# Subtracting the low halves of the inner groups on POOL instead of DVE, in a chain of attention and two mixtures

## The chip, the cores and the metric

One Trainium2 chip, one core of it. The metric is the device time of one execution in microseconds; for the kernel before, the median of three runs is 637.03 us (636.54 to 637.32).

## The reference

An attention-like scan over 4 x 8 heads of 768 positions, then two feed-forward layers over the 3072 tokens of 256 features:

```python
x = attn_out.transpose(0, 2, 1, 3).reshape(B * S, H * D)      # 3072 x 256
h = x @ w_in                                                  # 256 -> 2048
g = maximum(h, 0) + alpha * minimum(h, 0)
x = g @ w_out                                                 # 2048 -> 256
gate = 1 / (1 + exp(-(x @ w_gate)))                           # 256 -> 1536
out = (gate * (x @ w_val)) @ w_out2                           # 1536 -> 256
```

## The kernel before, in words

All matrix products of the two layers are made in pieces, to keep float32 accuracy: each operand is split into a high half, which is a rounded copy, and a low half, which is the operand minus that copy. A product is then high x high, low x high and high x low. The weights are split once, in seven small operations per block (`work`, lines 142 to 185, called through `feed`); their raw words come by DMAs issued from POOL's queue (`take_up`, line 126), each of which waits until the buffer of an earlier block is free, that is until DVE has done line 181 of that block.

Tokens go in 6 blocks of 512, named `k`; the inner features go in groups of 128, named `f`. One step (k, f) of the first mixture has on PE six matmuls into `h` (`moe1_in`, line 429), on ACT the first half of the activation (`t`, line 434), on DVE the second half (`g`, line 436), and then `halves` (lines 441 to 452): ACT copies `g` into the high half `gh` (line 449), DVE subtracts it and leaves the low half `gl` (line 450). `moe1_out` (line 473) gives `gh` and then `gl` to PE, four and two matmuls. In the second mixture the inner value is `p`, and `moe2_out` has lines 552 (with `gh`) and 557 (with `gl`).

The order of the work is written out by hand, and each engine takes its instructions strictly in that order. There are three stages:

- The attention, in 32 chunks of 96 positions, into which the first 26 steps of the first mixture are woven; these call `halves` at line 935.
- The loop of lines 979 to 1003: the other steps of the first mixture and the first block of the second, 82 steps. Step i has `halves` of step i - 1, the inner products of step i and the outer products of step i - 2 (`LAG = 2`), then two weight operations. `halves` is called at line 981.
- `moe2_pair` (lines 659 to 736), for the blocks k = 1 to 5 of the second mixture, six pairs of groups j = 0 to 5 for each: 30 calls. It makes the inner products of two groups with seven products instead of eight, into the PSUM banks `a`, `b` and `c`, with DVE forming sums between them (lines 681, 694, 695, 718, 721) and the two values `p0` (lines 696 and 727) and `p1` (line 725). `halves(before[0])` of line 686 splits the previous pair's `p0` in the middle of a pair, before `moe2_out` of it; `halves(keys[1])` of line 733 splits `p1` at the end of its pair. The last pair of all splits in pieces (lines 708 and 729 to 731).

Some pairs have more: j = 1 sends the previous block's output (`send`: line 568 on DVE); j = 1 and 2 split the next block's input (line 421), j = 3 and 4 form differences of it (line 653), and the pair j = 5 splits those (`t_split`, line 657), the last of the four at its end, line 735, so that it runs when the next block's first pair has begun.

In the timelines, the `gl` of the row `L450 gl<-g` belongs to a step of the first mixture, that of `gl<-p` to the second.

Of the kernel before, what the change touches and what calls it, by code (L numbers as in the profile page):

```python
# [12 lines left out]
ALU = mybir.AluOpType  # L13
# [11 lines left out]
BL = 512  # L25
# [22 lines left out]
def kernel(  # L48
# [21 lines left out]
    nc = tc.nc  # L70
# [20 lines left out]
    bf = lambda t: t.bitcast(F32)  # L91
# [98 lines left out]
    def feed(n, groups):  # L190

        for _ in range(n):
            if worked[0] < ready(groups - 1):
                work()
# [9 lines left out]
    for j in range(F2 // WG):  # L204
        cs = slice(j * WG, (j + 1) * WG)
# [208 lines left out]
    def split_x(kind, k, lo=0, hi=BL):  # L414

        if lo == 0:
            xh[kind, k] = ring.tile([128, 2, KT, BL], F32R, tag="xs", name="xh", bufs=2)
        t = xh[kind, k][:, :, :, lo:hi]
        src = x1[:, :, k * BL + lo:k * BL + hi]
        nc.scalar.copy(t[:, 0], src)  # L420
        nc.vector.tensor_tensor(t[:, 1], src, bf(t[:, 0]), op=ALU.subtract)
# [16 lines left out]
        )  # L438
        gt["m1", k, f] = g

    def halves(key, lo=0, hi=BL):

        if lo == 0:
            gh = ring.tile([128, BL], F32R, tag="gh", name="gh", bufs=3)
            gl = ring.tile([128, BL], F32R, tag="gl", name="gl", bufs=3)
            gt[key] = gt[key], gh, gl
        g, gh, gl = gt[key]
        cs = slice(lo, hi)
        nc.scalar.copy(gh[:, cs], g[:, cs])  # L449
        nc.vector.tensor_tensor(gl[:, cs], g[:, cs], bf(gh[:, cs]), op=ALU.subtract)  # L450
        if hi == BL:
            gt[key] = gh, gl

# [110 lines left out]
    def send(k, e):  # L564

        sides(k, e)
        sb = ring.tile([128, 2, DM], F32, tag="mag", name="osb", bufs=3)
        nc.vector.tensor_tensor(sb, po[k][e][:, :, 0:DM], side.pop(e), op=ALU.add)
        r0 = k * BL + e * 256
        nc.sync.dma_start(  # L570
            out=out[r0:r0 + 256, :].rearrange("(u p) d -> p u d", p=128), in_=sb
        )
# [33 lines left out]
    def product(bank, k, j, a, b, first):  # L606

        for e in range(2):
            for i, (wl, xl) in enumerate(((1, 0), (0, 0), (0, 1))):
                nc.tensor.matmul(  # L610
                    bank[:, e], left_of(e, j, a, wl), right_of(k, b, xl),
                    start=first and e == i == 0, stop=i == 2, skip_group_check=True,
                )
# [30 lines left out]
    def t_sum(k, i):  # L644

        if i == 0:
            tf[k] = ring.tile([128, 4, 256], F32, tag="raw", name="tf", bufs=RAWS)
        b = lambda kt, u: x1[:, kt - 1, k * BL + (u - 1) * 256:k * BL + u * 256]
        t = tf[k]
        p, q = (  # L650
            (b(1, 2), b(1, 1)), (b(2, 2), t[:, 0]), (b(2, 2), b(1, 2)), (b(2, 1), t[:, 1])
        )[i]
        nc.vector.tensor_tensor(t[:, i], p, q, op=ALU.subtract)

    def t_split(k, t):
        nc.scalar.copy(t_of(t, 0), tf[k][:, t])
        nc.vector.tensor_tensor(t_of(t, 1), tf[k][:, t], bf(t_of(t, 0)), op=ALU.subtract)

    def moe2_pair(k, j, before):

        tt = nc.vector.tensor_tensor
        end = j == F2 // WG - 1
        more = end and k + 1 < NBK
        final = end and k + 1 == NBK
        two = lambda t: t.rearrange("p (e u) -> p e u", e=2)
        a = two(psum.tile([128, BL], F32, tag="h", name="pa"))
        b = two(psum.tile([128, BL], F32, tag="y", name="pb"))
        if j % 2 == 0:
            vt[k] = psum.tile([128, 2, BL], F32, tag="cb", name="pc")
        c = two(vt[k][:, j % 2])  # L670
        cs = ring.tile([128, 2, 2, 256], F32, tag="raw", name="cs", bufs=RAWS)
        u2 = ring.tile([128, 2, 2, 256], F32, tag="raw", name="u2", bufs=RAWS)[:, 0]
        s0, s1 = (ring.tile([128, BL], F32, tag="s", name="s") for _ in range(2))
        p0, p1 = (ring.tile([128, BL], F32, tag="g", name="p") for _ in range(2))
        lo, hi = slice(0, 256), slice(256, 512)

        product(a, k, j, "A11", "B11", True)
        product(b, k, j, "S2", "T2", True)
        product(c, k, j, "S1", "T1", True)
        nc.scalar.copy(cs[:, :, 0], a)  # L680
        tt(u2, b, cs[:, :, 0], op=ALU.add)
        if j == 1:
            for e in range(2):
                send(k - 1, e)
        if before[0] not in whole:
            halves(before[0])
        if more:
            t_split(k + 1, 1)
        product(a, k, j, "A12", "B21", False)
        product(b, k, j, "S3", "T3", False)  # L690
        nc.scalar.activation(s0[:, lo], a[:, 0], AF.Sigmoid)
        if more:
            t_split(k + 1, 0)
        tt(cs[:, :, 1], b, cs[:, :, 0], op=ALU.add)  # L694
        tt(cs[:, :, 1], c, cs[:, :, 1], op=ALU.add)
        tt(p0[:, lo], a[:, 1], s0[:, lo], op=ALU.mult)
        if more:
            t_split(k + 1, 2)
        elif j in (1, 2) and not final and k + 1 < NBK:
            split_x("m2", k + 1, (j - 1) * 256, j * 256)  # L700
        elif j in (3, 4) and k + 1 < NBK:
            for t in range(2):
                t_sum(k + 1, 2 * (j - 3) + t)
        f = 2 * j
        keys = [("m2", k, f), ("m2", k, f + 1)]
        gt[keys[0]], gt[keys[1]] = p0, p1
        if final:
            halves(keys[0], 0, 256)
        moe2_out(*before[0][1:])
        last = ("c", "b") if final else ("b", "c")  # L710
        for w in last:
            if w == "b":
                product(b, k, j, "A22", "T4", False)
            else:
                product(c, k, j, "S4", "B22", False)
        for w in last:
            if w == "b":
                tt(cs[:, :, 0], b, cs[:, :, 0], op=ALU.add)  # L718
                nc.scalar.activation(s1, cs[:, 0].rearrange("p u c -> p (u c)"), AF.Sigmoid)  # L719
            else:  # L720
                tt(u2, c, u2, op=ALU.add)
                nc.scalar.activation(s0[:, hi], u2[:, 0], AF.Sigmoid)
        for w in last:
            if w == "b":
                tt(p1, cs[:, 1].rearrange("p u c -> p (u c)"), s1, op=ALU.mult)  # L725
            else:
                tt(p0[:, hi], u2[:, 1], s0[:, hi], op=ALU.mult)
        if final:
            halves(keys[0], 256, 512)
            halves(keys[1], 0, 256)  # L730
            halves(keys[1], 256, 512)
        else:
            halves(keys[1])
        if more:
            t_split(k + 1, 3)
        moe2_out(*before[1][1:])
# [8 lines left out]
    with tc.manual_schedule():  # L745
        steps = [("m1", k, f) for k, f0, f1 in segs for f in range(f0, f1)]
# [4 lines left out]
        def step_in(i, tag):  # L751
            kind, k, f = steps[i]
            (moe1_in if kind == "m1" else moe2_in)(k, f, tag)

        def step_out(i, **kw):
            kind, k, f = steps[i]
            (moe1_out if kind == "m1" else moe2_out)(k, f, **kw)

        def splits(i):

            if i + 5 < len(steps):
                kind, k, f = steps[i + 5]
                if f == 0 and (kind, k) not in (("m1", 0), ("m1", 1)):
                    split_x(kind, k)
# [212 lines left out]
            moe1_done(steps[at - 2][1])  # L977
        plain = nm1 + NF2
        for i in range(at, plain):
            if i - 1 < len(steps):  # L980
                halves(steps[i - 1])
            m1 = i < nm1
            step_in(i, (("h", "y", "cb") if m1 else ("h", "y"))[i % (3 if m1 else 2)])
            if i - LAG >= out_at:
                step_out(i - LAG)
            feed(2, len(queue) if i > last1 + 3 else kept)
            if i + 5 < plain:
                splits(i)
            if i >= nm1:
                f = i - nm1  # L990
                if f == 0:
                    todo.append(NF2 // 2 - 2)
                if f in (4, 6):
                    split_x("m2", 1, (f - 4) * 128, (f - 2) * 128)
                if f == 8:
                    for t in range(4):
                        t_sum(1, t)
                if f == NF2 - 2:
                    for t in (1, 0, 2, 3):
                        t_split(1, t)  # L1000
                if f % 2 and f < NF2 - 1:
                    todo.append(f // 2 if f < NF2 - 3 else NF2 // 2 - 1)
                sum_up(5)
# [88 lines left out]
```

## Time and profile before

| | |
|---|---|
| median of three runs | 637.03 us |
| the profiled execution | 638.78 us |
| its span, from first to last instruction | 637.0 us |
| PE busy | 625.9 us, 98% |
| DVE busy | 520.4 us, 82% |
| ACT busy | 364.7 us, 57% |
| POOL busy | 39.4 us, 6% |
| granted TensorE clock, mean | 0.997 |
| chain that ended last | PE 92%, ACT 3%, DVE 2% |

The busy times are those of one profiled execution, which took 1.8 us more than its span. The granted clock is the share of full speed that the TensorE had. The chain that ended last is the work followed back from the last instruction, at each step to what released it.

### The profile page before, as it was taken

How to read it: one execution, taken by the hardware profiler on the slowest of the kernel's cores; microseconds unless marked ns; L12 is line 12 of the kernel's file. 1: busy time of each engine (PE TensorE's matmuls, PEld its weight loads, DVE VectorE, ACT ScalarE, POOL GpSimd, SP SyncE). 2: the span in 40 equal slices, each digit the busy share in tenths (PEclk: the TensorE clock that was granted, in tenths of full speed). 3: DMA queues.
4: the chain of work that ended last, by engine and by line, in shares of the span. 5: the costliest groups of instructions: out<-in, count | busy, mean ns of one | idle time of the engine just before them, and what ended most of it. 6: DMA issues, size and time to landing. Idle time of an engine off the chain costs nothing.

```text
span 637.0 us, 11146 instructions
## 1 busy us (share of the span) xinstructions
PE 625.9 (98%) x4336; PEld 519.1 (81%) x4336; DVE 520.4 (82%) x910; ACT 364.7 (57%) x729; POOL 39.4 (6%) x68
## 2 busy tenths in 40 slices
PE   8799999999999999999999999999999999999997
PEld 4356666667888888888888888999999999999996
DVE  7799988865888878777676988888888888888876
ACT  7788877865666666566555435534534534534443
POOL 9211001000000000000000000000000000000000
PEclk9899999999999999999999999999999999999999
DMA  6744334410221221220000000100100100100100
GB/s 189 223 143 157 113 117 123 132 44 2 67 66 34 66 67 34 66 66 1 1 1 1 1 1 1 34 1 2 34 1 1 35 1 2 34 1 2 34 1 33
DMA packets 19270, 30.69 MB, mean 48 GB/s; under 512 B 7330, under 2 KB 14658, under 8 KB 19218
## 3 DMA queue, kind: packets, MB, share of 16 engines
q0 software_dynamic: 5232, 18.44, 9.2%
q1 hardware_dynamic: 13474, 11.08, 6.1%
q8 instruction: 34, 0.56, 0.4%
q10 hardware_dynamic: 512, 0.47, 0.2%
q14 instruction: 18, 0.15, 0.1%
HBM read 26.57 MB, written 3.34 MB: 47 GB/s over the span
## 4 chain that ended last, share of the span: by engine, by line
PE 92%; ACT 3%; DVE 2%; DMA 1%; issue 1%; POOL 0%; ACTq 0%; DVEq 0%
PE acc L473 21%; PE h L429 20%; PE pb L610 10%; PE po L552 10%; PE pa L610 7%; PE pc L610 7%; PE po L557 5%; PE cb L351 3%; PE gate L504 3%; PE val L504 3%; PE yd L386 1%; PE d L322 1%; DMA raw<-in_moe_w_in_dram 1%; PE yd L380 1%; ACT lt L337 1%
## 5 line engine op out<-in xcount | busy, mean ns | idle before, releaser
L429 PE MATMUL h<-xh,win 128*128 128x512 f32 x576 | 146.9, 390 | 0.5 <-ACT xh L420 0.5
L429 PEld LDWEIGHTS h<-xh,win 128*128 128x128 f32 x576 | 107.7, 188 | 22.3 <-ACT xh L420 0.8
L473 PE MATMUL acc<-gh,wout 128*128 128x512 f32 x384 | 105.8, 397 | 0.6 <-ACT x L398 0.6
L436 DVE SCALAR_TENSOR_TENSOR g<-h,salpha,t 128x512 f32<-128x512 f32 x96 | 71.9, 749 | 41.5 <-ACT t L434 41.2
L473 PEld LDWEIGHTS acc<-gh,wout 128*128 128x128 f32 x384 | 70.1, 188 | 27.0 <-ACT t L434 10.6
L434 ACT ACTIVATE t<-h,sign 128x512 f32<-128x512 f32 x96 | 66.0, 688 | 43.7 <-PE h L429 43.2
L449 ACT CAST gh<-g 128x512 fp32r<-128x512 f32 x96 | 59.7, 621 | 43.0 <-DVE g L436 43.0
L450 DVE TENSOR_TENSOR gl<-g,gh 128x512 fp32r<-128x512 f32 x96 | 66.0, 688 | 15.9 <-ACT gh L449 14.8
L719 ACT ACTIVATE s<-cs 128x512 f32<-128x512 f32 x30 | 19.0, 633 | 92.5 <-DVE cs L718 92.5
L552 PE MATMUL po<-w2out,gh 128*128 128x512 f32 x240 | 65.3, 394 | 0.0
L450 DVE TENSOR_TENSOR gl<-p,gh 128x512 fp32r<-128x512 f32 (+1 forms) x74 | 49.7, 672 | 12.6 <-ACT gh L449 12.6
L473 PE MATMUL acc<-gl,wout 128*128 128x512 f32 x192 | 59.2, 389 | 0.0
L449 ACT CAST gh<-p 128x512 fp32r<-128x512 f32 (+1 forms) x74 | 45.0, 610 | 20.8 <-DVE p L725 12.0
L552 PEld LDWEIGHTS po<-w2out,gh 128*128 128x128 f32 x240 | 41.8, 189 | 6.1
L610 PE MATMUL pa<-xh,w2in 128*128 128x256 f32 x300 | 44.0, 282 | 0.0
L473 PEld LDWEIGHTS acc<-gl,wout 128*128 128x128 f32 x192 | 36.0, 188 | 7.8
L557 PEld LDWEIGHTS po<-w2out,gl 128*128 128x128 f32 x240 | 36.3, 188 | 5.5 <-DVE gl L450 0.9
L610 PEld LDWEIGHTS pa<-xh,w2in 128*128 128x128 f32 x300 | 39.3, 190 | 0.0
L557 PE MATMUL po<-w2out,gl 128*128 128x256 f32 x240 | 38.0, 280 | 0.0
L337 ACT ACTIVATE lt<-d 112x768 f32<-112x768 f32 x32 | 26.0, 812 | 13.2 <-PE d L322 12.2
L694 DVE TENSOR_TENSOR cs<-pb,cs 128x512 f32<-128x512 f32 x30 | 20.7, 689 | 14.3 <-PE pb L610 14.3
L358 DVE TENSOR_TENSOR mt<-cb,lt 112x768 f32<-112x768 f32 x32 | 30.4, 949 | 0.2 <-ACT lt L337 0.2
(165 smaller groups left out, 1040.1 us busy)
## 6 DMA issues: line engine op xcount, KB each, us to landing
raw<-in_moe_w_out_dram POOLq DMA_DIRECT2D x14, 512.0 KB, 4.1
xs<-in_xb_dram SPq DMA_DIRECT2D x32, 144.0 KB
raw<-in_moe_w_in_dram POOLq DMA_DIRECT2D x8, 512.0 KB, 4.3
raw<-in_moe_w_gate_dram POOLq DMA_DIRECT2D x6, 512.0 KB, 4.1
raw<-in_moe_w_val_dram POOLq DMA_DIRECT2D x6, 512.0 KB, 4.1
out_dram<-osb SPq DMA_DIRECT2D x10, 256.0 KB
bt<-in_bc_dram SPq DMA_DIRECT2D x7, 192.0 KB
ct<-in_bc_dram SPq DMA_DIRECT2D x28, 48.0 KB
```

What stands on the lines that cost most here:

```text
L337: nc.scalar.activation(t.rearrange("j (e h) t -> j e (h t)", e=2), d[:, :, 0:4 * T], AF.Exp)
L358: nc.vector.tensor_tensor(m.rearrange(split, e=2), CBT.pop(c)[:, :, 0:4 * T].rearrange("j e (q t) -> j e q t", t=T), LT[c].rearrange(split ...
L429: nc.tensor.matmul(h, w[:, wl, kt, :], xh["m1", k][:, xl, kt, :], start=(i == 0 and kt == 0), stop=(i == 2 and kt == KT - 1),)
L434: nc.scalar.activation(t, h, AF.Identity, scale=sign[:, f:f + 1])
L436: nc.vector.scalar_tensor_tensor(g, h, salpha[:, f:f + 1], t, op0=ALU.mult, op1=ALU.max)
L449: nc.scalar.copy(gh[:, cs], g[:, cs])
L450: nc.vector.tensor_tensor(gl[:, cs], g[:, cs], bf(gh[:, cs]), op=ALU.subtract)
L473: nc.tensor.matmul(acc[k][:, m], w[:, wl, m * 128:(m + 1) * 128], g, start=(first and i == 0), stop=(last and i == 2),)
L504: nc.tensor.matmul(p, w[:, wl, kt, :], xh["m2", k][:, xl, kt, :], start=(i == 0 and kt == 0), stop=(i == 2 and kt == KT - 1),)
L552: nc.tensor.matmul(o[e][:, u].rearrange("p (l d) -> p l d", l=2), ph[:, ts], w, start=(f == 0), stop=False, skip_group_check=True,)
L557: nc.tensor.matmul(o[e][:, u, 0:DM], pl[:, ts], w[:, 0, :], start=False, stop=last, skip_group_check=True,)
L610: nc.tensor.matmul(bank[:, e], left_of(e, j, a, wl), right_of(k, b, xl), start=first and e == i == 0, stop=i == 2, skip_group_check=True,)
```

## The change

`halves` gets an argument, the engine of the subtraction, and three of its calls hand over POOL (`nc.gpsimd`): the one in the middle of a pair, the one at the end of a pair, and the one in the loop behind the attention. The calls during the attention, the one between the loop and the first pair, and those of the last pair's own groups keep DVE. The condition that goes with the last one was always true there.

```diff
-    def halves(key, lo=0, hi=BL):
+    def halves(key, lo=0, hi=BL, e=nc.vector):
...
         nc.scalar.copy(gh[:, cs], g[:, cs])
-        nc.vector.tensor_tensor(gl[:, cs], g[:, cs], bf(gh[:, cs]), op=ALU.subtract)
+        e.tensor_tensor(gl[:, cs], g[:, cs], bf(gh[:, cs]), op=ALU.subtract)
...
         if before[0] not in whole:
-            halves(before[0])
+            halves(before[0], e=nc.gpsimd)
...
         else:
-            halves(keys[1])
+            halves(keys[1], e=nc.gpsimd)
...
         for i in range(at, plain):
-            if i - 1 < len(steps):
-                halves(steps[i - 1])
+            halves(steps[i - 1], e=nc.gpsimd)
```

The order on PE, ACT and SP is the same as before. On POOL, in the loop behind the attention, the subtractions now stand between the DMAs that load raw weights (`raw` is the buffer of a block's raw words):

```order
 L126 DMA raw<-in_moe_w_gate_dram 128x2x512
+L450 TENSOR_TENSOR gl<-g,gh 128x512
 L126 DMA raw<-in_moe_w_val_dram 128x2x512
+L450 TENSOR_TENSOR gl<-g,gh 128x512 x4
 L126 DMA raw<-in_moe_w_out_dram 128x2x512
+L450 TENSOR_TENSOR gl<-g,gh 128x512 x3
```

The first subtraction on POOL stands alone in front of a DMA; the second, that of the next step, is behind that DMA, and so it goes on with three or four to a DMA.

On DVE, where a pair j = 0 and the pair j = 1 behind it meet (`cs` and `u` hold the sums, `pb` and `pc` are the banks `b` and `c`, `osb` is the output that is sent):

```order
 L725 TENSOR_TENSOR p<-cs,s 128x512
 L727 TENSOR_TENSOR p<-u_4823,s 128x256
-L450 TENSOR_TENSOR gl<-p,gh 128x512
 L681 TENSOR_TENSOR u_4909<-pb,cs 128x512
 L568 TENSOR_TENSOR osb<-po,side 128x512 x2
-L450 TENSOR_TENSOR gl<-p,gh 128x512
 L694 TENSOR_TENSOR cs<-pb,cs 128x2x256
 L695 TENSOR_TENSOR cs<-pc,cs 128x2x256
```

Both subtractions of the pair leave DVE: L681 follows L727, and L694 and L695 follow the sending.

On DVE, where the last pair of a block ends and the next block's first pair begins (`tf` holds the differences of the next block's input, `wout_80` is the home of one split of them):

```order
 L725 TENSOR_TENSOR p<-cs,s 128x512
 L727 TENSOR_TENSOR p<-u_4728,s 128x256
-L450 TENSOR_TENSOR gl<-p,gh 128x512
 L657 TENSOR_TENSOR wout_80<-tf,wout_80 128x256
 L681 TENSOR_TENSOR u_4823<-pb,cs 128x512
-L450 TENSOR_TENSOR gl<-p,gh 128x512
 L694 TENSOR_TENSOR cs<-pb,cs 128x2x256
```

The split L657 stays in front of L681, and the subtraction that stood in front of it is now POOL's.

## Rows read from the trace of the kernel before

**Rows 1.** The page: busy time, share of the span and instructions of each engine.

```profile
PE 625.9 (98%) x4336; PEld 519.1 (81%) x4336; DVE 520.4 (82%) x910; ACT 364.7 (57%) x729; POOL 39.4 (6%) x68
```

**Rows 2.** Stretches: us, busy us of each engine (instructions), clock, DMA share, GB/s.

```profile
440.00:480.00 40.00, 40.00 (x299) 38.06 (x298) 34.31 (x61) 17.57 (x37) 0.00 (x0) 1.00 0.04 14
```

**Rows 3.** Groups by line and shape: count | busy us, mean ns | idle before, releasers.

```profile
L450 DVE TENSOR_TENSOR gl<-g,gh 128x512 fp32r<-128x512 f32 x96 | 66.0, 688 | 15.9 <-ACT gh L449 14.8
...
L450 DVE TENSOR_TENSOR gl<-p,gh 128x512 fp32r<-128x512 f32 x70 | 48.1, 687 | 11.9 <-ACT gh L449 11.9
```

**Rows 4.** The same view, of POOL alone.

```profile
L790 POOL COPY xs<-eye 16x128 f32<-16x128 f32 x6 | 2.1, 382 | 0.1
...
L810 POOL TENSOR_SCALAR bt<-units 128x64 f32<-128x64 f32 x2 | 0.9, 448 | 0.6 <-DMA units<-in_k_misc_dram 0.5
```

**Rows 5.** Timeline (start, us, engine, line): a weight DMA and the next `gl`'s use.

```profile
264.69 0.72 POOL L126 DMA_DIRECT2D raw<-in_moe_w_gate_dram  x1 [10.57 <-ACT t L434]
...
267.02 0.62 PE L473 MATMUL acc<-gl,wout 128*128 128x512 f32 x2
```

**Rows 6.** Timeline: the first steps behind the attention.

```profile
154.33 0.69 DVE L450 TENSOR_TENSOR gl<-g,gh 128x512 fp32r<-128x512 f32 x1 [0.69 <-ACT gh L449]
...
158.22 0.62 PE L473 MATMUL acc<-gl,wout 128*128 128x512 f32 x2
...
159.56 0.72 POOL L126 DMA_DIRECT2D raw<-in_moe_w_val_dram  x1 [30.15 <-ACT mag L138]
...
160.94 0.62 PE L473 MATMUL acc<-gl,wout 128*128 128x512 f32 x2
```

**Rows 7.** Timeline: a plain pair; `gh` of `p1`, of `p0`, use, next pair.

```profile
605.38 0.88 PE L610 MATMUL pa<-xh,w2in 128*128 128x256 f32 x6
605.63 0.62 ACT L449 CAST gh<-p 128x512 fp32r<-128x512 f32 x1 [0.32 <-DVE p L725]
...
606.77 0.62 ACT L449 CAST gh<-p 128x512 fp32r<-128x512 f32 x1
...
609.90 0.63 PE L557 MATMUL po<-w2out,gl 128*128 128x256 f32 x4
...
613.20 0.88 PE L610 MATMUL pa<-xh,w2in 128*128 128x256 f32 x6
```

**Rows 8.** Timeline: a pair j = 1, which sends an output.

```profile
589.58 0.88 PE L610 MATMUL pa<-xh,w2in 128*128 128x256 f32 x6
...
591.93 0.64 ACT L449 CAST gh<-p 128x512 fp32r<-128x512 f32 x1
...
593.27 0.68 DVE L450 TENSOR_TENSOR gl<-p,gh 128x512 fp32r<-128x512 f32 x1
...
594.59 0.69 DVE L695 TENSOR_TENSOR cs<-pc,cs 128x512 f32<-128x512 f32 x1
...
597.55 0.88 PE L610 MATMUL pa<-xh,w2in 128*128 128x256 f32 x6
```

**Rows 9.** Timeline: the first pair of block 2, from `gh` of `p1` on.

```profile
440.66 0.62 ACT L449 CAST gh<-p 128x512 fp32r<-128x512 f32 x1 [0.43 <-DVE p L725]
...
441.92 0.42 DVE L657 TENSOR_TENSOR wout<-tf,wout 128x256 fp32r<-128x256 f32 x1
442.25 0.69 DVE L681 TENSOR_TENSOR u<-pb,cs 128x512 f32<-128x512 f32 x1
...
443.07 0.91 PE L610 MATMUL pb<-wout,win 128*128 128x256 f32 x6
```

**Rows 10.** POOL beside DVE: timeline, and line 365's ns min/median/max with first and last start.

```profile
13.78 0.29 POOL L790 COPY xs<-eye 16x128 f32<-16x128 f32 x1
...
14.01 0.28 DVE L365 TENSOR_TENSOR bd<-xs,lt 112x128 f32<-112x128 f32 x1
14.01 0.43 POOL L790 COPY xs<-eye 16x128 f32<-16x128 f32 x1
...
L365 DVE TENSOR_TENSOR bd<-xs,lt x28: 275/280/284, 10.8 to 141.8; 112x128 f32<-112x128 f32 x28
```

## The prediction, made before the changed kernel ran

> **What bounds the kernel.** I read the page's busy line first: PE is busy for 625.9 of 637.0 us, DVE for 520.4, POOL for 39.4 [rows 1]. PE's missing 11 us lie almost wholly in the attention and in the tail, which the change leaves alone. The stretch table shows it: between 440 and 480 us PE is busy for 40.00 of 40.00 us at a granted clock of 1.00, while DVE has 5.7 us to spare [rows 2]. So after the attention PE alone sets the pace, and taking work off DVE is worth only what PE still loses there to a late DVE. I looked for such losses in the timeline. In the pair stage (30 calls of `moe2_pair`) a plain pair takes 613.20 - 605.38 = 7.82 us from its first product to the next pair's [rows 7]. The pair that also sends the last block's output (j = 1, five of them) takes 597.55 - 589.58 = 7.97 [rows 8]. Its DVE runs two more subtractions of the output's size, and L695, which PE's product `c` waits for, starts only at 594.59. That is 0.15 us, five times: 0.7 us is all that the trace offers.
>
> **What the change removes.** 140 of the 170 subtractions of line 450 go from DVE to POOL: 71 of the form `gl<-g` and 69 of the form `gl<-p`, 688 and 687 ns each [rows 3], 96 us of DVE time. It is worth the 0.7 us above, since DVE's L694 and L695 of the sending pairs start without an L450 in front of them. Everywhere else the saved DVE time is idle time.
>
> **What it adds: how long is one on POOL?** No row shows a two-input operation on POOL. Below, it can hardly be shorter than DVE's own 0.69 us. Above, POOL's TENSOR_SCALAR takes 448 ns for 64 elements [rows 4], eight times that is 3.6 us. The nearest row is the COPY, SBUF to SBUF as ours: 382 ns on average for 128 elements [rows 4], 0.29 us at its quickest [rows 10]; four times that is 1.2 to 1.5 us, and I take 1.3 us, since a longer operation spreads what is fixed but reads a second input. The Trainium skill, GPSIMD Engine Reference, section 3.1 (Elementwise), gives 4497 ns for such an addition of 2048 elements; a quarter, 1.1 us, would be an estimate by that page.
>
> **Does the longer subtraction reach PE?** Three places.
> - Inner steps of the first mixture. A `gl` is used two steps after it is made, so by itself 0.6 us more reaches nothing. But POOL's queue also holds 14 weight DMAs in this stretch, each of which waits for DVE's L181 and has the next `gl` behind it. The tightest, the twelfth, is issued at 264.69 and takes 0.72; 1.3 behind that is 266.71, and PE takes that `gl` at 267.02 [rows 5]: 0.3 us left, and no stall. The DMAs themselves are put off by at most one `gl`; from the first at 159.56 [rows 6] to the twelfth they are 9.6 us apart, and their weights are worked on three blocks later, so that costs nothing. In the first block of the second mixture the lag is the same two steps and a step carries more matmuls, so there is more room.
> - The first step after the attention. There PE has one group of matmuls less between a step and its use. The DMA is issued at 159.56, ends at 160.28, and the `gl` behind it ends at 161.58, but PE wants it at 160.94 [rows 6]. That is a stall of 0.6 us, once. (By the page's 1.1 us it would be 0.4 us.)
> - The pairs. POOL has two subtractions in a row: that of `p1`, whose `gh` ends at 606.25, and that of `p0`, whose `gh` ends at 607.39; PE takes the `gl` of `p0` at 609.90 [rows 7]. 606.25 + 2 x 1.3 = 608.85, so a microsecond is left. In a sending pair `gh` of `p0` comes late, at 591.93 + 0.64 = 592.57; 1.3 us later is 593.87, and DVE's own delivery was no earlier, 593.27 + 0.68 = 593.95 [rows 8].
>
> **The sum.** -0.7 + 0.6 = -0.1 us, nothing. The profiled execution took 638.78 us (span 637.0) and stays there; the median of the three runs was 637.03, and I predict 637.0. About 0.2%, 1.3 us, is what a measurement of this kernel can tell from no change.
>
> **Rivals.**
> *DVE held off by POOL (slower).* The trace shows that the two engines share something: POOL's COPY took 0.29 us at 13.78, but 0.43 at 14.01, when DVE's L365, two SBUF inputs, began beside it; L365 itself is 0.28 there and between 275 and 284 ns in all 28 places [rows 10]. So POOL paid, and DVE did not. The Trainium skill says more: SBUF — State Buffer, section Who interferes with whom, has a DVE instruction with two SBUF inputs and a POOL instruction that reads SBUF exclude each other for the whole instruction, and the one that starts second waits. This trace agrees on the sharing; that DVE is ever the one to wait behind a POOL read, no row of it shows. If so, one place decides. At the start of k = 2 to 5, the first pair runs the split L657 (two SBUF inputs) on DVE, in front of L681, which PE's second product `b` waits for; L657 starts at 441.92, L681 at 442.25 and PE goes on at 443.07 [rows 9]. POOL's `gl` of `p1` would begin when `gh` ends, at 440.66 + 0.62 = 441.28, before L657 is ready, and end at 442.58. L657 is then 0.66 us late, L681 too, and PE starts 0.13 us after L681's end now (442.94 to 443.07), which is the hand-over: 0.66 us, four times, 2.6 us. The stall after the attention may grow by another 0.5, where L421 and L164 stand on DVE. Result: 637.0 + 2.6 = 639.6. It decides from 0.2 us of hold-off on. For it: the shared cost above, and the page. Against it: DVE's unmoved 0.28 us. All other two-input operations of the pair stage (L725, L727, L421, L653) stand where POOL has already finished.
> *POOL too slow (slower).* The two subtractions of a pair have 609.90 - 606.25 = 3.65 us, less what PE needs to load and the engines to hand on, say 3.3: at 1.65 us each, POOL becomes the bound. At 2.0 us it would be 2 x 2.0 - 3.3 = 0.7 us in each of 29 pairs, 20 us: 657. Only the TENSOR_SCALAR row speaks for this, and it is a short one with a broadcast input.
> *The first call costs extra (slower).* The first `gl` on POOL can start where DVE's did, at 154.33, and PE takes it at 158.22 [rows 6]; with 1.3 us of its own, whatever holds it for more than 2.6 us is a stall. No row shows such a hold. The Trainium skill, GPSIMD Engine Reference, section 2.1 (Instruction dispatch), gives about 6 us for the first call of a freshly loaded kernel, which the profile would not show. With a hold of that size the stall would be 3.4 us and the time 640.4.
> *A faster DVE helps PE after all (faster).* It would need more than 1.3 us of PE loss, and the trace has 0.7 to give. Only attention and tail hold more, and they keep their subtractions.
>
> **How the numbers follow.** My forecast 0.52, from 636.3 (the start stall does not come) to 637.5; DVE held off 0.31; POOL too slow 0.09; the first call 0.05; faster 0.03. So within 0.2%: 0.52; slower: 0.31 + 0.09 + 0.05 = 0.45; faster: 0.03. The range runs from 636.1, the full gain with a little scatter, to 640.2, DVE held off with the extra 0.5 us; what is left out is mostly the slow POOL and the first call, some 0.15.
>
> **What would show it.** In the changed profile L450 stands on POOL with 140 instructions near 1.3 us, DVE's busy time is near 424 us, POOL's near 220. The period of a sending pair falls from 7.97 to 7.83; PE has a gap of 0.6 us near 161 us. If DVE is held off, L657 at the start of a block (around 441 us) lasts longer or starts late, and the pair that has it grows by 0.66 us. The prediction is wrong if POOL's L450 takes over 1.65 us, or if PE waits for `gl` or for DVE in most pairs or most inner steps.

## The result, and the profile after

The changed kernel takes 641.86 us (median of 4 runs, 641.39 to 643.64), the kernel before 636.90 us (4 runs, 636.54 to 637.32): a ratio of 1.0083 with a 95% interval of 1.0062 to 1.0103, 4 to 6.6 us slower. The forecast was 637.0 with a range up to 640.2, so the prediction was wrong. The profiled execution took 641.74 us, 640.0 us of it the span.

The busy line of the page, which answers to [rows 1], and the stretch of [rows 2]:

```profile
PE 627.1 (98%) x4336; PEld 518.1 (81%) x4336; DVE 475.6 (74%) x770; ACT 363.3 (57%) x729; POOL 227.9 (36%) x208
```

```profile
440.00:480.00 40.00, 39.55 (x293) 37.49 (x292) 28.56 (x50) 17.43 (x37) 12.94 (x10) 1.00 0.04 14
```

The move took place: 140 instructions went from DVE to POOL. But DVE's busy time fell by 44.8 us, not by the 96 us that those 140 took there [rows 3], and PE, which was busy for all of the 40 us from 440 to 480, now stands for 0.45 us of them.

How long the subtraction takes on POOL is in the view of line 450 (ns minimum/median/maximum, first and last start):

```profile
L450 POOL TENSOR_TENSOR gl<-g,gh x71: 1282/1299/1820, 152.0 to 343.8; 128x512 fp32r<-128x512 f32 x71
L450 POOL TENSOR_TENSOR gl<-p,gh x69: 1290/1300/1857, 347.6 to 626.2; 128x512 fp32r<-128x512 f32 x69
```

The median is 1.30 us, which is what the prediction took. Where DVE's time went is in the groups by line and shape (count | busy us, mean ns). Before:

```profile
L164 DVE TENSOR_SCALAR raw<-raw 128x512 uint32<-128x512 uint32 x26 | 11.0, 424 | 0.0
L421 DVE TENSOR_TENSOR xh<-x,xh 128x1024 fp32r<-128x1024 f32 x6 | 7.3, 1218 | 0.4 <-ACT xh L420 0.4
L625 DVE TENSOR_TENSOR msum<-w2in 128x1024 f32<-128x1024 f32 x5 | 6.1, 1218 | 0.0
...
L657 DVE TENSOR_TENSOR wout<-tf,wout 128x256 fp32r<-128x256 f32 x10 | 4.1, 416 | 0.0
```

After:

```profile
L164 DVE TENSOR_SCALAR raw<-raw 128x512 uint32<-128x512 uint32 x26 | 33.8, 1302 | 0.0
L421 DVE TENSOR_TENSOR xh<-x,xh 128x1024 fp32r<-128x1024 f32 x6 | 10.6, 1768 | 0.1
L625 DVE TENSOR_TENSOR msum<-w2in 128x1024 f32<-128x1024 f32 x5 | 10.5, 2093 | 0.0
L657 DVE TENSOR_TENSOR wout<-tf,wout 128x256 fp32r<-128x256 f32 x10 | 8.8, 888 | 2.6 <-ACT wout L656 2.6
```

The same instructions last longer. With the ten L657 of the other form (`win<-tf`), L626 and L628 these groups take some 43 us more than before, most of the 51 that are missing. Others kept their durations: L681 begins beside a subtraction of POOL in 29 of its 30 places and takes 0.69 us as before, and L694 and L436 are unchanged too. Each of those takes one of its inputs from PSUM.

**Where PE lost the time.** The two profiled executions left the attention 2.5 us apart, so I compare stretches behind it, by PE's own rows: from the first product into `acc` behind the attention (L473) to the first `gate` (L504), from there to the first `pa` of a pair, and from that to the `pa` of the thirtieth pair.

```
                     first mixture   2nd mixture, block 0   29 pairs
before                  190.52            49.40              228.00
after                   191.98            50.16              231.18
difference               +1.46            +0.76               +3.18   together 5.40
```

5.4 us lies inside the measured interval. The gain that was forecast is there, in the sending pairs of [rows 8]. The same pair after the change:

```profile
592.62 0.88 PE L610 MATMUL pa<-xh,w2in 128*128 128x256 f32 x6
...
596.41 0.69 DVE L694 TENSOR_TENSOR cs<-pb,cs 128x512 f32<-128x512 f32 x1
...
600.46 0.28 PE L610 MATMUL pa<-xh,w2in 128*128 128x256 f32 x1
```

600.46 - 592.62 = 7.84 us instead of 7.97, and nearly the same in all five: -0.65 together. The largest loss stands where [rows 9] stood, in the first pair of block 2:

```profile
440.48 0.88 PE L610 MATMUL pa<-xh,w2in 128*128 128x256 f32 x6
...
441.73 2.71 POOL L450 TENSOR_TENSOR gl<-p,gh 128x512 fp32r<-128x512 f32 x2 [5.46 <-ACT gh L449]
...
441.99 1.32 DVE L657 TENSOR_TENSOR wout<-tf,wout 128x256 fp32r<-128x256 f32 x1 [0.66 <-ACT wout L656]
...
443.23 0.68 DVE L681 TENSOR_TENSOR u<-pb,cs 128x512 f32<-128x512 f32 x1
...
443.96 0.98 PE L610 MATMUL pb<-wout,win 128*128 128x256 f32 x6 [0.45 <-DVE u L681]
```

POOL's subtraction begins at 441.73, L657 at 441.99, and L657 lasts 1.32 us instead of 0.42. It ends at 443.31, soon after the first of POOL's two must be over (441.73 + 1.30 = 443.03). L681 stands behind it, and PE's `pb` waits for L681. The pair takes 8.54 us instead of 7.85; those of blocks 2 to 5 lose 2.74 us together. The other losses in the pair stage are the first pair of block 1, 8.40 instead of 7.83, and the pairs j = 5 of blocks 1 to 4, 8.00 instead of 7.88, in which an L657 is held too.

The 0.76 us of block 0 are two waits of PE's product `val` for L511, in which DVE reads the `val` of the step before. The first of them, before the change:

```profile
356.26 0.68 DVE L511 TENSOR_TENSOR p<-val,s 128x512 f32<-128x512 f32 x1
...
357.28 1.52 PE L504 MATMUL val<-xh,w2in 128*128 128x512 f32 x6
```

After:

```profile
353.49 2.31 DVE L625 TENSOR_TENSOR msum<-w2in 128x1024 f32<-128x1024 f32 x1
...
355.73 0.68 DVE L511 TENSOR_TENSOR p<-val,s 128x512 f32<-128x512 f32 x1
...
356.46 1.23 PEld L504 LDWEIGHTS val<-xh,w2in 128*128 128x128 f32 x6 [0.48 <-DVE p L511]
```

Before, `val` begins 0.34 us after L511 has ended; now L511 stands behind an L625 that lasts 2.31 us, and PE's weight load for `val` waits for it.

### The profile page after: what moved, and what is told of

Its sections match the earlier page's. It is cut to its first block, busy times and chain, and to the rows that moved or that the text cites. A ratio compares the mean times of both kernels' runs of the same rounds, so it can differ in the third digit from the quotient of the medians.

```text
span 640.0 us, 11372 instructions
## 1 busy us (share of the span) xinstructions
PE 627.1 (98%) x4336; PEld 518.1 (81%) x4336; DVE 475.6 (74%) x770; ACT 363.3 (57%) x729; POOL 227.9 (36%) x208
## 4 chain that ended last, share of the span: by engine, by line
PE 74%; DVE 13%; ACT 6%; issue 5%; POOL 1%; DMA 1%; DVEq 0%; ACTq 0%; POOLq 0%
PE acc L473 20%; PE h L429 19%; PE pb L610 8%; PE po L552 6%; PE pa L610 5%; PE pc L610 5%; PE po L557 3%; PE cb L351 3%; ACT gh L449 2%; DVE msum L625 1%; PE d L322 1%; PE yd L386 1%; DVE p L511 1%; DVE p L725 1%; PE nobody L773 1%
## 5 line engine op out<-in xcount | busy, mean ns | idle before, releaser
L450 POOL TENSOR_TENSOR gl<-p,gh 128x512 fp32r<-128x512 f32 x69 | 90.9, 1330 | 191.6 <-ACT gh L449 187.8
L436 DVE SCALAR_TENSOR_TENSOR g<-h,salpha,t 128x512 f32<-128x512 f32 x96 | 71.9, 748 | 76.4 <-ACT t L434 69.4
L450 POOL TENSOR_TENSOR gl<-g,gh 128x512 fp32r<-128x512 f32 x71 | 96.9, 1372 | 84.1 <-ACT gh L449 82.0
L473 PE MATMUL acc<-gh,wout 128*128 128x512 f32 x384 | 105.8, 397 | 0.6 <-ACT x L398 0.6
L473 PEld LDWEIGHTS acc<-gh,wout 128*128 128x128 f32 x384 | 70.1, 188 | 27.0 <-ACT t L434 10.6
L473 PE MATMUL acc<-gl,wout 128*128 128x512 f32 x192 | 59.5, 391 | 0.8 <-POOL gl L450 0.8
L473 PEld LDWEIGHTS acc<-gl,wout 128*128 128x128 f32 x192 | 35.8, 188 | 9.4 <-POOL gl L450 1.6
L694 DVE TENSOR_TENSOR cs<-pb,cs 128x512 f32<-128x512 f32 x30 | 20.7, 690 | 27.2 <-PE pb L610 27.1
L681 DVE TENSOR_TENSOR u<-pb,cs 128x512 f32<-128x512 f32 x30 | 20.7, 689 | 24.2 <-PE pb L610 17.3
L164 DVE TENSOR_SCALAR raw<-raw 128x512 uint32<-128x512 uint32 x26 | 33.8, 1302 | 0.0
```

What stands on the lines that cost most here:

```text
L164: nc.vector.tensor_scalar(low, low, 29, None, op0=ALU.logical_shift_right)
L436: nc.vector.scalar_tensor_tensor(g, h, salpha[:, f:f + 1], t, op0=ALU.mult, op1=ALU.max)
L450: e.tensor_tensor(gl[:, cs], g[:, cs], bf(gh[:, cs]), op=ALU.subtract)
L473: nc.tensor.matmul(acc[k][:, m], w[:, wl, m * 128:(m + 1) * 128], g, start=(first and i == 0), stop=(last and i == 2),)
```

## Experiments

Theory H (held off): DVE instructions with two inputs in SBUF cannot run beside a POOL instruction that reads SBUF, and what waits for them on PE is late. Theory Q (queue): the low half itself comes late, since POOL is slower and has DMAs in its queue that wait. Each kernel starts from the changed one. The stretches of all, as in the table above:

```
                     first mixture   2nd mixture, block 0   29 pairs
e1_pairs_only           190.52            49.39              231.25
e2_loop_only            192.01            50.17              228.65
e3_split_free           191.97            50.20              228.80
e4_dma_from_sp          190.52            50.20              231.20
e5_write_only           192.77            49.40              227.50
e6_split_first          191.95            50.19              227.77
e7_twice                191.98            50.20              231.20
e8_quiet_pairs          190.49            49.40              227.40
```

**Only the pairs, only the loop.**

```diff
-            halves(steps[i - 1], e=nc.gpsimd)
+            halves(steps[i - 1])
```

> Only the 58 subtractions of the pairs are on POOL; those of the loop behind the attention are back on DVE. Theory H (DVE held off: a DVE instruction with two SBUF inputs, or the shift of line 164, waits until POOL's subtraction beside it has ended): the pair stage keeps its loss of 3.2 us less the 0.6 us that the loop's last steps hand to its first pair, so before plus 2.6 us, 639.5. Theory Q (queue: PE waits for a low half that is late because POOL is slower and has weight DMAs in front of it, nobody is held off): no DMA is issued in the pairs, so the loss goes with the loop, at most 637.5.

```diff
-            halves(before[0], e=nc.gpsimd)
+            halves(before[0])
...
-            halves(keys[1], e=nc.gpsimd)
+            halves(keys[1])
```

> Only the 82 subtractions of the loop behind the attention are on POOL; the pairs have theirs on DVE. Theory H: before plus the loop's part, two stalls in the first mixture (1.4 us), some in the first block of the second (0.75) and in the first pair (0.6), 2.7 us in all, 639.6. Theory Q: the whole loss of 5 us, 641.5 or more.

Measured: 640.04 us (ratio 1.0051, 1.0036 to 1.0066) and 640.30 us (1.0053, 1.0038 to 1.0069). Each call site keeps the loss of its own stretch, and of the 0.65 us that the loop alone leaves in the pairs 0.57 are the first pair of block 1 (8.41), which the loop's last subtraction runs into. The parts come to 0.7 us more in the pairs than the whole (3.25 and 0.65 against 3.18): in e1 two pairs, 8.29 in block 1 and 8.87 at the start of block 5, take 0.3 us more than in the changed kernel, with a hand-over between ACT and DVE that came 0.3 us later. No other run has these two, and their cause is open. In the pairs Q is out, since 637.5 was its most. The loop's interval, 639.2 to 641.2, holds H's 639.6 and not Q's 641.5; but H's figure took in the two stalls of the first mixture, so this run doesn't say whose those are.

**The split free of POOL.** The subtraction of `p1` in the last pair of a block goes back to DVE, so that none runs on POOL when L657 comes.

```diff
-            halves(keys[1], e=nc.gpsimd)
+            halves(keys[1], e=nc.vector if more else nc.gpsimd)
```

> As the change, but in the last pair of each of the blocks 1 to 4 the subtraction for p1, the one that stood beside the split L657 of the next block's first pair, is on DVE: 4 of 140 subtractions go back. Theory H: the four first pairs fall from 8.53 us to 7.85, 2.8 us less than the change, 639.1. Theory Q: no difference that can be measured, 641.9.

Measured: 639.79 us (1.0049, 1.0034 to 1.0064). The first pairs of blocks 2 to 5 take 7.93 instead of 8.54, where 7.85 was expected; nothing else changed. Four instructions on another engine take 2.4 us off the pair stage.

**The order alone.** The four instructions stay on POOL, but the last L657 is issued ahead of them, and with it its copy on ACT (L656), which now stands in front of the copy that makes `gh`.

```diff
+            if more:
+                t_split(k + 1, 3)
             halves(keys[1], e=nc.gpsimd)
-        if more:
-            t_split(k + 1, 3)
```

> The last L657 of a block is put ahead of the subtraction of p1 in the last pair of the block, on DVE's order ahead of nothing else that moves. DVE held off: L657 no longer falls beside the first subtraction, the first pairs of k = 2 to 5 go from 8.53 back to about 7.85, run 641.9 - 2.7 = 639.2. Late low half: first pairs stay 8.53, run 641.9.

Measured: 639.39 us (1.0035, 1.0021 to 1.0048). L657 now starts as soon as L727 is done, before ACT has `gh` ready for POOL:

```profile
441.48 0.42 DVE L657 TENSOR_TENSOR wout<-tf,wout 128x256 fp32r<-128x256 f32 x1
441.96 2.54 POOL L450 TENSOR_TENSOR gl<-p,gh 128x512 fp32r<-128x512 f32 x2 [5.46 <-ACT gh L449]
...
442.40 0.69 DVE L681 TENSOR_TENSOR u<-pb,cs 128x512 f32<-128x512 f32 x1 [0.51 <-ACT cs L680]
```

The first pairs are at 7.83. POOL does exactly the same work as in the changed kernel, and the loss of 2.8 us is gone. The overlap caused it, not the length of the subtraction. The first pair of block 1 fell from 8.40 to 7.83 too, which this edit doesn't touch: 0.57 of the 3.4 us that the pair stage gained. The last section comes back to that.

**POOL writes but doesn't read.** In place of each of POOL's subtractions stand three writes of a constant, so the low halves of 140 groups are left out.

```diff
-        e.tensor_tensor(gl[:, cs], g[:, cs], bf(gh[:, cs]), op=ALU.subtract)
+        if e is nc.vector:
+            e.tensor_tensor(gl[:, cs], g[:, cs], bf(gh[:, cs]), op=ALU.subtract)
+        else:
+            for n in (512, 512, 256):
+                e.memset(bf(gl[:, 0:n]), 0.0)
```

> Leaves out the low halves of the 140 groups that POOL had: three writes of a constant stand in their place (512, 512 and 256 columns), near 1.3 us together and with nothing read. DVE held off by what POOL reads: L657, L421 and L625 are back to 0.42, 1.1 and 1.2 us, the 29 pairs of the pair stage take 227.4 us (before 228.0, less 0.65 in the sending pairs), the second mixture's first block 49.4; the stalls behind the DMAs of the loop may stay (191.9 for the rest of the first mixture, before 190.5). Whole run near 637.7. A late low half on POOL, or POOL busy by itself: pairs still 231.2, run 641.9.

Measured: 638.94 us (1.0024, 1.0012 to 1.0035). POOL is even busier, 235.8 us, the three writes taking 1.42 us together. The pair stage takes 227.50 us, 0.5 less than before the change, and the block ahead of it 49.40, as before. The groups there, whose line numbers are four higher (L629 is L625, L661 is L657):

```profile
L164 DVE TENSOR_SCALAR raw<-raw 128x512 uint32<-128x512 uint32 x26 | 15.1, 582 | 0.0
...
L629 DVE TENSOR_TENSOR msum<-w2in 128x1024 f32<-128x1024 f32 x5 | 6.1, 1219 | 0.0
...
L661 DVE TENSOR_TENSOR wout<-tf,wout 128x256 fp32r<-128x256 f32 x10 | 4.1, 420 | 2.6 <-ACT wout L660 2.6
```

Writes start without waiting for `gh`, so they don't stand at quite the same moments as the subtractions. They do fall beside the two-input instructions, and cost them nothing. Nor is it that one write, some 0.55 us, is shorter than a subtraction: in 54 places a two-input instruction begins when 0.15 to 0.55 us of a write are still to run, and none lasts over 0.02 us longer than usual. One of them:

```profile
361.51 1.49 POOL L454 MEMSET gl<- 128x512 f32 x3 [2.64 <-PE po L561]
361.99 1.22 DVE L629 TENSOR_TENSOR msum<-w2in 128x1024 f32<-128x1024 f32 x1
```

The same pair of neighbours in the changed kernel:

```profile
359.71 1.67 POOL L450 TENSOR_TENSOR gl<-p,gh 128x512 fp32r<-128x512 f32 x1 [0.64 <-ACT gh L449]
360.14 2.32 DVE L625 TENSOR_TENSOR msum<-w2in 128x1024 f32<-128x1024 f32 x1
```

So it is POOL's reading of SBUF that holds off these instructions. The Trainium skill, SBUF — State Buffer, section Who interferes with whom, says just this: a DVE instruction with two SBUF inputs contends with a POOL instruction that reads SBUF, "not with one that only writes it". The runs agree, with 1.22 us beside a write and 2.32 beside a read. What stayed in this run is the loss in the first mixture, 192.77 us: PE's stalls behind two DMAs are still there, and larger (1.16 and 0.85 us), and 0.2 us came up behind a third, the one that the prediction took for the tightest. That is 0.9 us more than was expected there, most of the 1.2 us by which the run missed its 637.7.

**The DMAs off POOL's queue.** From the end of the attention the raw weights are issued by SP.

```diff
-            nc.gpsimd.dma_start(
+            (nc.sync if behind else nc.gpsimd).dma_start(
...
+        behind.append(1)
```

> As the change, but the 14 weight DMAs of the loop behind the attention are issued from SP's queue instead of POOL's. Theory Q: PE's two stalls behind a DMA (0.6 us at the start of the loop, 0.75 some 20 us later) go, and with them the loss, 637 to 638. Theory H with the queue as a small part: those two stalls go, 1.4 us less than the change, 640.5, and the first pairs of the blocks stay at 8.5 us; the shift of line 164 is held for one subtraction, up to 1.3 us, no longer for 3.

Measured: 641.56 us (1.0067, 1.0051 to 1.0084). The whole time barely tells it from the changed kernel, since the attention scatters by more than what is at stake, but the first mixture takes 190.52 us again, as before the change: its 1.46 us went with the DMAs. The changed kernel's timeline at the second of its two stalls shows how:

```profile
173.87 0.62 ACT L449 CAST gh<-g 128x512 fp32r<-128x512 f32 x1 [0.89 <-DVE g L436]
...
175.66 0.69 DVE L181 SCALAR_TENSOR_TENSOR mag<-mag,raw 128x512 uint32<-128x512 uint32 x1
...
176.65 0.73 POOL L126 DMA_DIRECT2D raw<-in_moe_w_gate_dram  x1 [2.83 <-DVE mag L181]
176.94 3.29 DVE L164 TENSOR_SCALAR raw<-raw 128x512 uint32<-128x512 uint32 x1
...
177.40 2.52 POOL L450 TENSOR_TENSOR gl<-g,gh 128x512 fp32r<-128x512 f32 x2
...
178.75 0.74 PE L473 MATMUL acc<-gl,wout 128*128 128x512 f32 x2 [0.46 <-POOL gl L450]
```

`gh` was ready at 174.49, but POOL stood at the DMA, which waits for L181, until 176.35; the low half came 2.9 us late and PE waited. The same wait costs 0.62 us at the first step behind the attention. With the DMAs on SP, POOL takes the second place's `gl` when it is ready:

```profile
175.65 1.29 POOL L450 TENSOR_TENSOR gl<-g,gh 128x512 fp32r<-128x512 f32 x1 [1.37 <-ACT gh L449]
...
177.52 0.69 DVE L181 SCALAR_TENSOR_TENSOR mag<-mag,raw 128x512 uint32<-128x512 uint32 x1
...
178.79 0.42 DVE L164 TENSOR_SCALAR raw<-raw 128x512 uint32<-128x512 uint32 x1
179.46 0.62 PE L473 MATMUL acc<-gl,wout 128*128 128x512 f32 x2
```

The `gl` of 175.65 waited for its `gh` alone and is done before L181 begins, and PE takes it at 179.46 without a wait. In this run L164 is hardly held any more either, so by itself it doesn't say which of the two cost PE the time. The run with writes does: there L164 is held by 0.46 us at most, and the stalls behind the DMAs stayed. Block 0 of the second mixture and the pairs kept their loss here. So there are two mechanisms: Q in the first mixture, H behind it.

**The hold doubled.** The subtraction of `p1` in the last pair of a block is issued twice.

```diff
-    def halves(key, lo=0, hi=BL, e=nc.vector):
+    def halves(key, lo=0, hi=BL, e=nc.vector, times=1):
...
-        e.tensor_tensor(gl[:, cs], g[:, cs], bf(gh[:, cs]), op=ALU.subtract)
+        for _ in range(times):
+            e.tensor_tensor(gl[:, cs], g[:, cs], bf(gh[:, cs]), op=ALU.subtract)
...
-            halves(keys[1], e=nc.gpsimd)
+            halves(keys[1], e=nc.gpsimd, times=2 if more else 1)
```

> The subtraction of p1 is issued twice on POOL in the pairs before another pair, with the same result. DVE held off for as long as POOL reads: L657 waits 1.3 us longer, the first pairs of k = 2 to 5 go from 8.53 to about 9.8 and k = 1 too, 5 x 1.3 = 6.5, run near 648; plain pairs have 1.0 us of room for 1.3 more and grow by up to 0.3 each. A hold-off of fixed length: first pairs stay 8.53, run 642 to 648 by the plain pairs alone.

Measured: 644.01 us (1.0101, 1.0079 to 1.0124), and the pair stage 231.20. My expectation of 9.8 us for the first pairs of blocks 2 to 5 was wrong: they take 8.68. The timeline says why (line numbers here are one higher behind line 450):

```profile
442.70 3.96 POOL L451 TENSOR_TENSOR gl<-p,gh 128x512 fp32r<-128x512 f32 x3 [5.46 <-ACT gh L449]
...
442.96 1.31 DVE L658 TENSOR_TENSOR wout<-tf,wout 128x256 fp32r<-128x256 f32 x1 [0.66 <-ACT wout L657]
```

POOL now runs three subtractions in one go, and L658 still lasts 1.31 us: it ends 444.27 - 442.70 = 1.57 us after POOL's start, which is one subtraction and 0.27, and in the changed kernel, where POOL had two, this was 443.31 - 441.73 = 1.58. The two-input instruction gets in between POOL's first and second. It is held for what is left of one POOL instruction, not for POOL's whole work. The 0.15 us that the pair did lose are a late `gl` of `p0`, the third of the three: POOL ends at 446.66, and PE's weight load of that `gl`, at 446.71, had waited 0.30 us for it.

The run's median is 2 us above the changed kernel's while its stretches behind the attention are the same. In the pairs that is chance: these four lose 0.6 us more, and the first pair of block 1, 7.83 here as in e6, loses 0.57 less. In the profiled executions 1.5 us lie ahead of the first stretch, in the attention (it ends at 152.12, not 150.62), which the edit doesn't touch.

**The gain without the loss.** POOL keeps only the subtractions of the pairs that have no L657, 50 in all; those of the last pair of blocks 1 to 4 and of the loop are DVE's again.

```diff
-            halves(before[0], e=nc.gpsimd)
+            halves(before[0], e=nc.vector if more else nc.gpsimd)
...
-            halves(keys[1], e=nc.gpsimd)
+            halves(keys[1], e=nc.vector if more else nc.gpsimd)
...
-            halves(steps[i - 1], e=nc.gpsimd)
+            halves(steps[i - 1])
```

> Only the last pair's subtraction of the pair before and nothing of the loop nor of the other pairs stays on POOL where no L657, L625 or loop work is near: the loop's calls and those of the j = 5 side of the pairs go back to DVE. DVE held off: stages before the pairs as before (190.5 and 49.4), first pairs 7.85, sending pairs 7.84 instead of 7.97, run 636.9 - 0.65 = 636.2. Late low half: same as before or slower, 637 or more.

Measured: 636.36 us over 11 runs, the kernel before 637.05 over 27, ratio 0.9990 (0.9979 to 1.0001). No DVE instruction behind the attention lasts over 0.12 us longer than before:

```profile
L164 DVE TENSOR_SCALAR raw<-raw 128x512 uint32<-128x512 uint32 x26 | 11.1, 425 | 0.0
...
L657 DVE TENSOR_TENSOR wout<-tf,wout 128x256 fp32r<-128x256 f32 x10 | 4.1, 419 | 0.0
```

The pair stage takes 227.40 us, 0.6 less than before, all of it in the sending pairs. The whole time agrees with -0.65 but its interval just reaches no change, so as a faster kernel it is likely, not shown.

## Why the prediction was wrong

- **The gain**, -0.7 us: right, 0.65.
- **The duration**, 1.3 us: right, 1.30 at the median, and partly by luck: the mean of 382 ns that gave the upper bound holds copies of 0.43 and 0.61 us that ran beside DVE instructions, and four times the 0.29 of a free one is 1.16. POOL too slow is out, and so is a first call that costs extra: the first subtraction on POOL, at 152.0, is within the group's 1.28 to 1.82 us, and the stall behind it is the DMA's.
- **The stall behind the attention**, +0.6 us: right, 0.62, by the mechanism given (a DMA ahead of the low half). The extra 0.5 us that the rival saw there didn't come, though L164 lasts 3.21 us at that place.
- **The DMAs of the loop**, no stall: wrong in one of 14, +0.75. The step that failed is "The tightest, the twelfth, is issued at 264.69". It goes from each DMA to the `gl` that follows it in time. The rows of the kernel before at the third DMA:

```profile
177.19 0.69 DVE L181 SCALAR_TENSOR_TENSOR mag<-mag,raw 128x512 uint32<-128x512 uint32 x1
...
177.80 0.68 DVE L450 TENSOR_TENSOR gl<-g,gh 128x512 fp32r<-128x512 f32 x1
...
178.43 0.72 POOL L126 DMA_DIRECT2D raw<-in_moe_w_gate_dram  x1 [9.04 <-ACT mag L138]
...
179.98 0.62 PE L473 MATMUL acc<-gl,wout 128*128 128x512 f32 x2
```

  The first `gl` after the DMA of 178.43 is DVE's of 179.83, and for that one there is room. But the `gl` that DVE made at 177.80, before the DMA, stood behind L181 in DVE's order; on POOL it stands behind the DMA, which waits for the same L181, and PE took it at 179.98. By the prediction's own sum, 178.43 + 0.72 + 1.3 = 180.45, this was 0.5 us too late. The other 0.25 us go with L181 itself, which begins 1.16 us after the start of PE's product with `gh` there and no longer 0.84. It is 1.15 to 1.21 in every run in which the L164 ahead of it lasts 2.7 us, and 0.85 with writes, where that L164 lasts 0.64. That the held L164 is the cause of this part is likely, not shown.
- **DVE held off**, a rival with 0.31: this is what happened, at the place named. Its price there, 4 x 0.66 = 2.6 us, measured 2.74. The step that failed is the weighing: "DVE's unmoved 0.28 us" was taken as evidence that DVE doesn't wait [rows 10]. That row has the two begin at the same 14.01, with POOL the one that grew; to the nanosecond the trace has DVE's L365 begin at 14.007 and POOL's copy at 14.012, so the one that came second paid. POOL's next copy, at 14.38, takes 0.61 us behind a DVE instruction of 14.21. The rows show who lost when DVE was first, not who loses when POOL is, and L657 starts 0.26 us after POOL here. A row that shows a shared resource and one loser was read as a rule on who loses.
- **The same mechanism elsewhere** was priced at nothing, with "All other two-input operations of the pair stage (L725, L727, L421, L653) stand where POOL has already finished" and "there is more room" for block 0 of the second mixture. The four that are named are indeed never beside POOL. But the list leaves out the other L657: in each pair j = 5 of blocks 1 to 4 one of them stands beside POOL's subtraction of the previous pair's `p0` (+0.51 in four pairs). And in the first mixture and block 0 the weight work is full of such instructions: L421, L625, L626, L628, and L657 in the last step, worth +0.76 in the block and +0.57 in the first pair behind it. The room was counted for `gl`, but it was DVE's L511, behind a held L625 or L626, that PE waited for.

Together: -0.65 + 0.62 + 0.75 + 2.74 + 0.51 + 0.76 + 0.57 = 5.3 of the 5.4 us. The forecast had the first two; the rival had the 2.74; 2.6 us no case had.

## What to carry to other kernels

Work that is moved from DVE to POOL isn't free of DVE: before moving it, list every DVE instruction with both inputs in SBUF (and every one-input operation that was seen to be held) that can start while POOL reads, and ask which of them somebody waits for. Here moving four L657 out of POOL's reach (e6) was worth 2.8 us, and the DVE time that was saved 0.65. And when an operation goes to a queue that also issues waiting DMAs, walk that queue in its own order: the `gl` behind a DMA is the next one in program order, not the next one by the old engine's times.

## What was not expected of the hardware

- L164 is a DVE operation with one input, and it was held longest: 0.42 us before, up to 3.29 after. In the fence at 176.94 above it goes through the rest of a DMA's issue (to 177.38) and both subtractions behind it (to 179.92). In seven more of its places with two subtractions in one go it lasts 2.57 to 2.77 us. In nine of ten such places it didn't get in between the two, as L657 did; in one, at 207.69, it did and lasts 1.24 us. Beside POOL's writes alone it is still held, though by at most 0.46 us (0.58 us on average). The Trainium skill, SBUF — State Buffer, section Who interferes with whom, lists tensor_scalar among the operations that can run in a mode that takes the port pair shared with POOL, and then one of the two waits for the other's whole instruction; the rows fit that, for reads and for writes. Why it mostly misses the gap between two subtractions stays open. It costs PE little here: L164 was held in 14 of its 17 places behind the attention, and PE lost time in the first mixture at two places only, each by waiting for a `gl` behind a DMA.
- POOL waits too. In the last step ahead of the pairs, the run with L657 first (e6) has three DVE instructions in a row run at their usual length and POOL's one subtraction last 2.83 us:

```profile
391.22 0.75 DVE L657 TENSOR_TENSOR wout<-tf,wout 128x256 fp32r<-128x256 f32 x2
391.50 2.83 POOL L450 TENSOR_TENSOR gl<-p,gh 128x512 fp32r<-128x512 f32 x1 [2.88 <-ACT gh L449]
391.89 0.42 DVE L631 TENSOR_TENSOR wout<-sf,wout 128x256 fp32r<-128x256 f32 x1
392.23 0.95 DVE L633 TENSOR_TENSOR wout<-sf,wout 128x768 fp32r<-128x768 f32 x1
```

  In the changed kernel, with the same instructions in the same order and POOL again 0.28 us behind the first L657, POOL came first:

```profile
390.41 1.85 DVE L657 TENSOR_TENSOR wout<-tf,wout 128x256 fp32r<-128x256 f32 x2
...
390.69 1.29 POOL L450 TENSOR_TENSOR gl<-p,gh 128x512 fp32r<-128x512 f32 x1 [2.88 <-ACT gh L449]
```

  The first pair of block 1 takes 7.83 us in the one case and 8.40 in the other. Six runs have this step with the loop's subtraction on POOL: in the changed kernel, e2, e3 and e4 POOL began 0.279 to 0.282 us behind the first L657 and came first, in e6 and e7 it began 0.282 and 0.288 us behind it and came second. So it is close to a tie, and what decides it is open; 0.57 us of the loss can come and go with no change near it.
